# The last four zero pieces as four unequal transfers in a cached-attention training step

## The chip, the cores and the metric

The kernel runs on one core of a Trainium2 chip. The metric is the device time of one execution in microseconds. A measurement is the median of several runs of the kernel before, taken on the same chip as the kernel that it is compared with.

## The reference

Two layers of attention over a cache, each followed by an MLP, for one token of width 1024, forward and backward. The forward pass reads only the last 4096 of 32768 cache rows of each of 4 heads; the gradients of the caches therefore have 28672 rows of zeros for each head, and these must be written as well.

```python
W = min(4096, max(256, Sk // 4))                       # 4096 of Sk = 32768
k = jnp.repeat(k_cache[:, :, Sk - W:, :], rep, axis=1)
v = jnp.repeat(v_cache[:, :, Sk - W:, :], rep, axis=1)
p = _softmax(jnp.einsum("bhqd,bhkd->bhqk", q, k) * (Dh ** -0.5), axis=-1)
...
x = x + _A_ref(_layernorm(x), A_k_cache, A_v_cache, A_wq, A_wo)
x = x + _B_ref(_layernorm(x), B_w1, B_b1, B_w2)        # act = h * tanh(softplus(h))
x = x + _A_ref(_layernorm(x), A_k_cache, A_v_cache, A_wq, A_wo)
x = x + _B_ref(_layernorm(x), B_w1, B_b1, B_w2)
...
_out, _vjp = jax.vjp(_f, A_x, A_k_cache, A_v_cache, A_wq, A_wo, B_w1, B_b1, B_w2)
_grads = _vjp(grad_out)                                # out_1 .. out_8
```

out_2 and out_3 are the gradients of the key and the value cache, (1, 4, 32768, 128) in bf16. out_4, out_5, out_6 and out_8 are the gradients of the weight matrices wq, wo, w1 and w2.

## The kernel before

All matrices are streamed from memory in tiles of 128 partitions, most of them 1 MB (8 KB per partition), by DMAs that SP issues; a small planner (`Ring`) keeps a list of wanted tiles and issues the next one as soon as a slot is free. TensorE computes matrix times vector products and transposes, VectorE and ScalarE evacuate PSUM and compute row products. The weight matrices are passed several times: forward for both layers, backward for both.

The gradients of the weights and of the last 4096 cache rows are outer products. They are made late, in `units_rows`, `units_cols` and `units_kv`: two or four matmuls into a PSUM bank pair, one evacuation by VectorE or ScalarE (`evac`, which picks the engine with the smaller load), and a store of half a stage or the rest of it by SP (`store`, L1050 and L1055). Four lists (`todo`) are served in turn by `work`.

The zeros of out_2 and out_3 are written by POOL's own DMA queue. `zjobs` holds 56 jobs: for each of the two outputs and four heads, the 28672 zero rows are seen as 128 partitions of 224 rows, and these as seven pieces of 4096 elements (8 KB) per partition, 1 MB in all. Half of the first piece is written by SP, the other half goes to the end of the list. `zeros(n, after)` (L257) issues the next n jobs; with `after` given, POOL first copies one element of that tile, so that it waits until the tile is there. The calls stand all along the program: after o of the second forward layer, and at many points of the backward pass. The source is always `zt`, a tile of zeros with 4096 elements on each partition.

The backward pass of the first attention layer is the last pass that reads weights: wo (`do1`), then wq (`dn1(t)`, called for each of the eight row blocks t). In it `zeros(2, dnp[...])` stands at t == 3 (L1219), and the last call, `zeros(4)` (L1228), stands behind the whole pass: three whole pieces and the half. After it no zeros are left; the rest of the program makes and stores gradients.

Other transfers of POOL's queue lie between. `take_back` (L836) reads vectors of the forward pass back from a scratch in memory: AC as two transfers of 28 rows of 256 bytes, then OC (2 x 32 rows), NB and NA (2 x 8 rows each). `rows_go(nc.gpsimd)` (L1041) moves rows inside SBUF: four transfers of 8 rows of 256 bytes, two of 7 rows of 1024 bytes. In the profiled execution they are issued between 276.9 and 304.2 us.

Of the kernel before, what the change touches and what calls it, by code (L numbers as in the profile page):

```python
# [15 lines left out]
P = 128  # L16
HQ = 32
DH = 128
# [3 lines left out]
G = 4  # L22
# [71 lines left out]
def kernel(  # L94
# [22 lines left out]
    nc = tc.nc  # L117
# [3 lines left out]
    ZR = Sk - W  # L121
# [9 lines left out]
    def sb(shape, dtype, name):  # L131
        return keep.tile(shape, dtype, name=name)
# [24 lines left out]
    ZC = 4096  # L157
    zt = sb([P, ZC], BF16, "zt")
# [36 lines left out]
    for hi in range(4):  # L195
        r = slice(32 * hi, 32 * hi + 32)
# [49 lines left out]
    zjobs = []  # L246
    for out_t in (out_2, out_3):
        for g in range(G):
            dst = out_t[0, g, 0:ZR, :].rearrange("(p r) d -> p (r d)", p=P).rearrange("p (r c) -> p r c", c=ZC)
            for k in range(dst.shape[1]):  # L250
                zjobs.append(dst[:, k, :])
    zjobs.reverse()

    pz = sb([1, 16], FP32, "pz")
# [2 lines left out]
    def zeros(n, after=None):  # L257

        if after is not None and zjobs:
            nc.gpsimd.tensor_copy(pz[0:1, pz_n[0] % 16:pz_n[0] % 16 + 1], after[0:1, 0:1])  # L260
            pz_n[0] += 1
        for _ in range(n):
            if zjobs:
                dst = zjobs.pop()
                nc.gpsimd.dma_start(dst, zt[:, 0:dst.shape[1]])  # L265


    KEEP_Q = (5, 6, 7)
# [534 lines left out]
    def last_da(k):  # L803

        for c in (5, 6):
            if k == 0:
                da_dots(c)
            else:
                ring.release(("2", 0, c))
        if k:  # L810
            nc.gpsimd.memset(zt[:], 0.0)
            zeros(1)

    def wo_hook1(c):
        if c == 0:
            zeros(7, OC[:, 0, 1:2])
        if c:
            conv(1)
# [20 lines left out]
    put_by("OC", OC, HQ)  # L839
    put_by("NA", NA, TD)  # L840
    zeros(8, x3)
    sB1 = mlp_fwd(1, x3, st3, lambda: conv(1, "A"))
    put_by("NB", NB, TD)
# [381 lines left out]
            todo[0].append(units_cols(0, 8, out_4))  # L1225

    g0_rest = attn_bwd(0, sA0, g1, ("o", 3), ("q", 3), (), dict(do=do1, dp=dp1, dq=dq1, dn=dn1))
    zeros(4)  # L1228
    stage_free.extendleft(ring_t[:, i, :] for i in range(8))
    stage_free.extendleft(lent)  # L1230

# [50 lines left out]
```

## Time and profile before

| | us |
|---|---|
| median of three runs | 450.59 (450.19 to 450.88) |
| the profiled execution | 450.31 |
| its span, first to last instruction | 448.5 |
| PE busy | 314.8 (70%) |
| DVE busy | 262.2 (58%) |
| ACT busy | 209.4 (47%) |
| POOL busy | 44.5 (10%) |
| DMA: 181.40 MB | 404 GB/s on the mean |
| zeros by POOL: 55 pieces of 1 MB, one of 0.5 MB | first 114.2, last 331.6 (issue) |

The profile is a page with the busy time of each engine, the span in 40 slices with the share of busy DMA engines, the costliest groups of instructions and the DMA issues. The trace behind it answers questions on stretches of time: which instruction ran when, what it waited for, how busy the DMA engines were. It also holds every DMA packet with its start, length, queue and bytes (not its engine), and the 16 steps by which each transfer signals its end, one for each DMA engine.

### The profile page before, as it was taken

Reading aid. Unit: us, or ns where it says so; the run is one execution under the profiler, and the core shown is the slowest. Engines: PE = TensorE matmul, PEld = TensorE weight load, DVE = VectorE, ACT = ScalarE, POOL = GpSimd, SP = SyncE. Lnnn points to the kernel's source line nnn. Section 1 sums busy time; section 2 is a strip of 40 time slices with the busy share of each in tenths; the row PEclk is TensorE's granted clock in tenths of the full one; section 3 lists DMA queues with packets and bytes.
Section 4 is the critical chain, followed back from the end, with each engine's and each line's share of the span. In section 5 each row is a group of like instructions: output and inputs, shape, how many; then the busy total and the mean of one; then the engine's idle time right before and its main releaser. Section 6 shows DMA issues by size and latency. Waiting matters only on the chain.

```text
span 448.5 us, 12849 instructions
## 1 busy us (share of the span) xinstructions
PE 314.8 (70%) x5681; PEld 243.3 (54%) x5681; DVE 262.2 (58%) x516; ACT 209.4 (47%) x238; POOL 44.5 (10%) x94
## 2 busy tenths in 40 slices
PE   3835542565698797987987666798877888899600
PEld 3735532445685696986986545798862222234300
DVE  4504746368551664864477447654478998998600
ACT  2501101011058576861474341561348999999700
POOL 1000000001232212102101003023220000000000
PEclk9955555556559799986799657957685555555555
DMA  8999999999999999999999999999999899999994
GB/s 336 422 420 420 419 419 418 418 355 425 400 422 421 422 422 416 397 422 422 424 422 422 427 423 419 405 410 388 405 397 412 347 411 416 416 420 411 409 406 192
DMA packets 30057, 181.40 MB, mean 404 GB/s; under 512 B 3954, under 2 KB 5162, under 8 KB 12082
## 3 DMA queue, kind: packets, MB, share of 16 engines
q1 hardware_dynamic: 21478, 122.30, 66.6%
q0 software_dynamic: 8432, 58.26, 31.5%
q8 instruction: 44, 0.72, 0.6%
q14 instruction: 11, 0.09, 0.0%
q10 hardware_dynamic: 92, 0.02, 0.0%
HBM read 81.84 MB, written 98.62 MB: 402 GB/s over the span
## 4 chain that ended last, share of the span: by engine, by line
DMA 40%; PE 31%; DVE 13%; ACT 5%; issue 4%; SPq 0%; ACTq 0%; DVEq 0%
DMA ring<-in_B_w_dram 13%; PE BIG L489 10%; DMA W<-in_A_wo_dram 9%; DMA ring<-in_A_wq_dram 7%; DMA ring<-in_A_wo_dram 5%; DMA W<-in_B_w_dram 4%; PE TP L508 4%; PE wide L1129 4%; ACT ring L316 3%; PE wide L1078 3%; DVE ring L313 3%; DMA W<-in_A_k_cache_dram 2%; DVE W L313 2%; PE BIG L667 2%; PE MV L956 2%
## 5 line engine op out<-in xcount | busy, mean ns | idle before, releaser
L316 ACT COPY ring<-BIG 128x1024 bf16<-128x1024 bf16 x52 | 51.4, 1014 | 50.0 <-PE BIG L489 30.2
L1078 PE MATMUL wide<-W 2*128 2x512 bf16 x240 | 53.1, 597 | 9.7 <-ACT ring L316 2.4
L489 PE MATMUL BIG<-ident_bf,ring 128*128 128x128 bf16 x672 | 54.5, 234 | 2.0 <-issue 1.2
L489 PEld LDWEIGHTS <-ring 128*128 128x128 bf16 x768 | 51.6, 107 | 3.4 <-issue 2.7
L466 DVE CUSTOM_DVE_ANT_0 junk<-ring,SC 128x1024 bf16<-128x1024 bf16 x32 | 38.9, 1215 | 11.0 <-DMA ring<-in_B_w_dram 10.6
L1078 PEld LDWEIGHTS <-W 2*128 2x128 bf16 x240 | 12.8, 102 | 46.3 <-issue 45.4
L508 PEld LDWEIGHTS <-ring 128*128 128x128 bf16 x864 | 29.9, 98 | 11.7 <-issue 6.3
L316 ACT CAST ring<-wide 128x1024 bf16<-128x1024 f32 (+1 forms) x37 | 34.5, 1015 | 1.1 <-PE wide L1078 1.1
L265 POOL DMA_DIRECT2D out_dram<-zt x56 | 29.9, 538 | 48.8 <-DMA out_dram<-zt 47.9
L313 DVE CAST ring<-wide 128x1024 bf16<-128x1024 f32 (+1 forms) x27 | 31.3, 1198 | 2.8 <-PE wide L1078 2.7
L316 ACT COPY KT<-BIG 128x1024 bf16<-128x1024 bf16 x22 | 21.6, 1007 | 21.8 <-PE BIG L667 19.9
L313 DVE COPY ring<-BIG 128x1024 bf16<-128x1024 bf16 x32 | 21.8, 689 | 15.1 <-PE BIG L489 12.5
L466 DVE CUSTOM_DVE_ANT_0 junk<-ring,DSX 128x1024 bf16<-128x1024 bf16 x24 | 29.4, 1224 | 0.8
L489 PE MATMUL BIG<-ident_bf,W 128*128 128x128 bf16 x280 | 26.9, 255 | 3.1 <-DMA W<-in_A_wo_dram 2.7
L316 ACT COPY W<-BIG 128x1024 bf16<-128x1024 bf16 x20 | 20.1, 1014 | 11.8 <-PE BIG L489 11.6
L551 PE MATMUL MV<-NA,ring 128*128 128x1 bf16 x512 | 15.3, 165 | 13.4 <-DMA ring<-in_A_wq_dram 12.1
L489 PEld LDWEIGHTS <-W 128*128 128x128 bf16 x288 | 21.6, 123 | 3.5 <-DMA W<-in_A_wo_dram 2.9
L551 PEld LDWEIGHTS <-ring 128*128 128x128 bf16 x512 | 14.7, 104 | 14.2 <-DMA ring<-in_A_wq_dram 12.8
L1129 PE MATMUL wide<-W 32*128 32x256 bf16 x128 | 19.7, 403 | 1.5 <-DVE KT L313 0.9
L316 ACT CAST KT<-wide 128x1024 bf16<-128x1024 f32 x19 | 19.1, 1030 | 1.6 <-PE wide L1129 1.1
L316 ACT CAST W<-wide 128x1024 bf16<-128x1024 f32 x16 | 16.0, 1024 | 6.6 <-PE wide L1078 6.2
L354 PE MATMUL YR<-ring,AC 128*32 128x256 bf16 x208 | 10.9, 367 | 11.1 <-DMA ring<-in_B_w_dram 8.7
(279 smaller groups left out, 524.5 us busy)
## 6 DMA issues: line engine op xcount, KB each, us to landing
out_dram<-zt POOLq DMA_DIRECT2D x55, 1024.0 KB, 20.7
ring<-in_A_wq_dram SPq DMA_DIRECT2D x24, 1024.0 KB, 12.8
ring<-in_A_wo_dram SPq DMA_DIRECT2D x14, 1024.0 KB, 19.0
ring<-in_B_w_dram SPq DMA_DIRECT2D x13, 1024.0 KB, 18.9
W<-in_A_wo_dram SPq DMA_DIRECT2D x10, 1024.0 KB, 19.9
out_dram<-ring SPq DMA_DIRECT2D x15, 512.0 KB, 11.1
W<-in_B_w_dram SPq DMA_DIRECT2D x8, 896.0 KB, 18.4
out_dram<-ring SPq DMA_DIRECT2D x5, 1024.0 KB, 12.3
```

Of the source, the lines that this page charges most:

```text
L265: nc.gpsimd.dma_start(dst, zt[:, 0:dst.shape[1]])
L313: nc.vector.tensor_copy(dst, src)
L316: nc.scalar.copy(dst, src)
L354: nc.tensor.matmul(bank[32 * j:32 * j + 32, 0:n].rearrange("p (g a) -> p g a", a=m.shape[-1]), lhsT=vec.to_broadcast([P, 32]), rhs=m, star ...
L466: nc.vector.tensor_tensor_reduce(out=out, in0=a, in1=vec, scale=1.0, scalar=acc if i else 0.0, op0=ALU.mult, op1=ALU.add, accum_out=acc)
L489: nc.tensor.transpose(b[:, i * P:(i + 1) * P], block(w, i) if block else w[:, i * P:(i + 1) * P], ident_bf[:])
L508: nc.tensor.matmul(out, lhsT=w[:, i * P:(i + 1) * P], rhs=rhs_of(i), start=fresh[0], stop=last and i == n - 1, skip_group_check=True)
L551: nc.tensor.matmul(q_ps[:, h:h + 1], lhsT=ch[:, h * P:(h + 1) * P], rhs=NA[:, t, l:l + 1], start=(k == 0 and h == 0), stop=(k == TD - 1), ...
L667: nc.tensor.transpose(b[:, i * P:(i + 1) * P], T[:, g, 8 * b8 + i, :], ident_bf[:])
L956: nc.tensor.matmul(dq_ps[:, g_ * 8:g_ * 8 + 8], lhsT=KT[:, g_, t, :], rhs=DSX[:, c:c + 8], start=(g_ == 0 and t == 0), stop=(t == TS - 1), ...
L1078: nc.tensor.matmul(b[:, 512 * i:512 * i + 512], lhsT=R[at:at + 2, lo:lo + P], rhs=R[at:at + 2, ro + 512 * i:ro + 512 * i + 512], start=Tru ...
L1129: nc.tensor.matmul(b[:, k * 256:(k + 1) * 256], lhsT=RT[32 * g:32 * g + 32, a, tp, :], rhs=YS[32 * g:32 * g + 32, :], start=True, stop=Tru ...
```

## The change

The seven pieces of the last head of out_3 are cut in another way. The first 512 units of 32 rows (8 KB each, 4 MB in all) are set aside as `zless`; the other 384 units become three whole pieces. The list has 52 jobs then, so the call at t == 3 takes the last whole piece and the half piece, and the last `zeros(4)` becomes `zeros_less()`: four transfers of 4 x 33, 1 x 17, 3 x 33 and 8 x 33 units. Each of the 16 shares reads one partition of `zt` (0, 4, 8, 12; 16; 20, 24, 28; 64, 68 to 92), over and over, and writes one contiguous stretch of the output.

```diff
     zjobs = []
     for out_t in (out_2, out_3):
         for g in range(G):
-            dst = out_t[0, g, 0:ZR, :].rearrange("(p r) d -> p (r d)", p=P).rearrange("p (r c) -> p r c", c=ZC)
-            for k in range(dst.shape[1]):
-                zjobs.append(dst[:, k, :])
+            rest = out_t[0, g, 0:ZR, :]
+            if (out_t, g) != (out_3, G - 1):
+                dst = rest.rearrange("(p r) d -> p (r d)", p=P).rearrange("p (r c) -> p r c", c=ZC)
+            else:
+                units = rest.rearrange("(u r) d -> u (r d)", r=ZC // DH)
+                zless, dst = units[0:4 * P], units[4 * P:].rearrange("(r p) c -> p r c", p=P)
+            zjobs += [dst[:, k, :] for k in range(dst.shape[1])]
     zjobs.reverse()
...
+    def zeros_less():
+
+        at = 0
+        for k, p, n in ((4, 0, 33), (1, 16, 17), (3, 20, 33), (8, 64, 33)):
+            nc.gpsimd.dma_start(zless[at:at + k * n].rearrange("(k n) c -> k n c", k=k),
+                                zt[p:p + 4 * k:4, None, :].to_broadcast([k, n, ZC]))
+            at += k * n
...
     g0_rest = attn_bwd(0, sA0, g1, ("o", 3), ("q", 3), (), dict(do=do1, dp=dp1, dq=dq1, dn=dn1))
-    zeros(4)
+    zeros_less()
```

## The prediction

> **What bounds the kernel now.** I read the page's slices first: the 16 DMA engines are full from start to end, whatever PE, DVE and ACT do.
>
> ```profile
> DMA  8999999999999999999999999999999899999994
> GB/s 336 422 420 420 419 419 418 418 355 425 400 422 421 422 422 416 397 422 422 424 422 422 427 423 419 405 410 388 405 397 412 347 411 416 416 420 411 409 406 192
> ```
>
> From slice 18 on only slice 32 (347 GB/s) and the last (192) lie far under the rest. Next the timeline at the end: the last evacuation ends at 423.6 us, SP issues the last store at 437.7, the span ends at 448.5. The end is the drain of the stores.
>
> ```profile
> 422.61 1.02 ACT L316 CAST W<-wide 128x1024 bf16<-128x1024 f32 x1
> ...
> 437.72 1.06 SPq L1050 DMA_DIRECT2D out_dram<-W  x1
> ```
>
> Then that drain in windows (from:to, length, the engines' busy times and counts, PE clock, DMA share, GB/s):
>
> ```profile
> 440.00:442.00 2.00, 0.00 (x0) 0.00 (x0) 0.00 (x0) 0.00 (x0) 0.00 (x0) 0.50 1.03 410
> 442.00:443.00 1.00, 0.00 (x0) 0.00 (x0) 0.00 (x0) 0.00 (x0) 0.00 (x0) 0.50 0.33 131
> 443.00:444.00 1.00, 0.00 (x0) 0.00 (x0) 0.00 (x0) 0.00 (x0) 0.00 (x0) 0.50 0.06 25
> 444.00:445.00 1.00, 0.00 (x0) 0.00 (x0) 0.00 (x0) 0.00 (x0) 0.00 (x0) 0.50 0.07 29
> 445.00:446.00 1.00, 0.00 (x0) 0.00 (x0) 0.00 (x0) 0.00 (x0) 0.00 (x0) 0.50 0.06 25
> 446.00:447.00 1.00, 0.00 (x0) 0.00 (x0) 0.00 (x0) 0.00 (x0) 0.00 (x0) 0.50 0.07 29
> ```
>
> A share of 0.06 is one engine in sixteen. From about 443.1 to 447.16 (the last packet record) one engine alone moves its part: 4.1 us of the span belong to one late engine, which I call S. 29 packets of 4 KB in that time give 0.155 us per 4 KB, 0.31 us for an 8 KB row.
>
> **Since when S is late.** Each transfer signals its end in 16 steps, one per engine. For the zero piece issued at 327.95 the fifteenth step is at 333.8, the last at 338.9; for the store issued at 436.5 they are 442.2 and 446.3. With zeros alone on the queues (163 to 185 us) the last step advances about 2.75 us per piece, the others 2.45. S therefore loses while zeros run and keeps its lag afterwards: after 355 us no zeros are left, and nothing lets S catch up, since it never idles. The other fifteen do idle:
>
> ```profile
> 352.00:354.00 2.00, 1.59 (x11) 0.46 (x8) 2.00 (x3) 1.79 (x4) 0.00 (x0) 0.50 0.80 309
> 354.00:356.00 2.00, 1.40 (x10) 0.35 (x8) 2.00 (x3) 2.00 (x4) 0.00 (x0) 0.50 0.73 291
> 356.00:358.00 2.00, 1.92 (x10) 0.46 (x10) 1.67 (x3) 2.00 (x3) 0.00 (x0) 0.50 0.71 285
> ```
>
> (0.20 + 0.27 + 0.29) x 2 us = 1.5 us, in which production of stores is the limit. So bytes given to or taken from S move the end at 0.31 us per row, down to the second latest engine (443.1); up to 1.5 us more on each of the others hides in that gap.
>
> **Part 1: the same bytes in another order.** The t == 3 step takes a piece and the half piece instead of two pieces; the four transfers carry 4 MB (512 rows of 8 KB, the diff's units) instead of 3.5 MB. Bytes in total and the count of 56 issues stay. POOL's last issues were
>
> ```profile
> 327.95 2.63 POOL L265 DMA_DIRECT2D out_dram<-zt  x5
> 331.60 0.53 POOL L265 DMA_DIRECT2D out_dram<-zt  x1 [1.02 <-DMA out_dram<-zt]
> ```
>
> and nothing follows on POOL. A transfer of 2 x 32 rows (W<-dr_OC) took 0.70 us to issue against 0.53; even at 1.5 us each the four would be out by 336 us, while earlier pieces keep the engines busy until about 337. Cost 0; without that cover it is the excess of the issue times, about 2 us, most of it inside the 1.5 us gap.
>
> **Part 2: who moves the rows.** Before, a piece has 128 partitions, 8 rows per engine: four pieces are 32 rows on each. The new shapes are 4, 3 and 8 shares of 33 rows, and one transfer of 17 rows. The trace has POOL transfers of both shapes, and the packet records of POOL's queue show where they went:
>
> - One counting dimension: W<-dr_AC, 28 rows of 256 B, came as 512 B on fourteen engines, two rows each, the same fourteen both times. The two seven-row transfers (L1041, 303 us) also came as seven pairs of 1024 B packets, each pair on one engine. I see no rotation in these.
> - Two dimensions, outer 2: W<-dr_OC, dr_NB and dr_NA. S's own sequence between 290.8 and 294.2 us, when only S still had POOL work, is 512, end, 512, end, 64, 64, end, 32, end, 2048, end. The 64 and 32 are fillers that engines without a share get (4 B per row). So S moved no part of OC or NB, but half of NA (2048 B of 4 KB). Three transfers, successive pairs of engines, S in the third.
>
> Applied to the change: the 17 rows have one counting dimension, so two go to each of eight engines and one to a ninth; they start with the engines of the seven-row transfers. S is among those seven (a pair of 1024 B packets at 313.9, after every other engine had signalled by 310.9), so S gets 2. The 4 + 3 + 8 shares go on from the engine behind the NA pair: fifteen engines in succession. One of sixteen stays without 33 rows, the one just before the start: the second engine of the NA pair. S is one of that pair.
>
> S as the first of the pair: 33 + 2 = 35 rows, 3 more than before, 3 x 0.31 = 0.93 us at the end. Fillers add at most 0.15 us (six packets of about 25 ns). Bound below: S now reads its 33 rows from another partition than its own eight; if what slows it by 12% (2.75 against 2.45) is tied to those partitions, it saves up to 0.12 x 33 x 0.31 = 1.2 us. So between -0.2 and +1.1 us; I take +0.9, the row that is measured on S without zeros.
>
> The Trainium skill, page "DMA: Bandwidth & Descriptors", section "Why a DMA increments its semaphore by 16 and not by 1", says that POOL transfers on fewer than 16 engines take successive engines from a rotating position, on as many as divide the outer dimension. By it 17 rows would go to one engine; it names exceptions that are spread over all 16, and the 28-row packets here are such a one. The same page, section "Latency and other measured facts", calls engines 7 and 15 the usual slow ones beside POOL transfers; here one engine is slow, and it took part in seven-row transfers, so I do not rest on that numbering.
>
> **The rivals.**
> 1. Forecast: S keeps a share of 33. No relief; 450.59 + 0.9 = 451.5 (450.4 to 451.7). For it: it holds for S first in the pair, and for either if the six small transfers between NA and the zeros (298 to 304 us) move the start, or if other runs start elsewhere. Against it: S second of the pair is as likely by the NA packets.
> 2. Faster: S is the second engine of the pair and gets 2 rows. 30 rows less are 9.3 us, more than its lag; it is enough from 14 rows less on (4.1 / 0.31). The end falls to the second latest engine, 443.1, whose 3 extra rows (0.9 us) hide in the gap of 1.5: 450.6 - 4.1 = 446.5 (446.0 to 447.4). Place and price are in the 443 to 447 windows.
> 3. The 17 rows stay on one engine that is not S: sixteen engines in succession, S gets 33, one row more: 450.59 + 0.3 = 450.9. The change then does not do what it says for S. Against it: the 28 rows in pairs.
>
> By the page's rule with the rotation starting at S's turn, S would get 17 rows, and the end would fall by the same 4.1 us as in rival 2. For that S would have to be fifth from the start, and the NA packets put it fifteenth or sixteenth.
>
> **How the numbers follow.** The profiled execution took 450.31 (span 448.5 and 1.8 around it), 0.28 under the median 450.59 of three; the differences above are added to the median. A measurement of this kernel tells about 0.2% (0.9 us) from no change. Forecast 0.53: slower 0.47, and 0.06 within 0.2% by the lower bound. Rival 2, which needs one place in the rotation and no shift: 0.39. Rival 3: 0.08, within 0.2%. So faster 0.39, same 0.14, slower 0.47. The predicted time is the forecast's, 451.5; its own range is 450.4 to 451.7. The range has to take in rival 2: 446.2 to 451.9.
>
> **What would show it.** Forecast: the one-engine stretch at the end (share 0.06) stays 4 to 5 us long, and S's last POOL packet comes about 1 us later than 355.05. Rival 2: no such stretch, the DMA share falls from 1 to 0 within about 1 us at 443, and POOL's queue is done on all engines before 350. Rival 3: the stretch is longer by 0.3. In all of them PE, DVE and ACT keep their times. I am wrong throughout if the dip at 352 to 358 or the issue of stores on SP moves by more than 1 us: then the end is not decided by S's bytes.

## The result, and the profile after

The changed kernel takes 458.11 us (median of six runs, 456.87 to 458.67) against 450.74 for the kernel before in the same comparison: ratio 1.016, 95% interval 1.0143 to 1.0177, 7.4 us slower. The forecast was 451.5 and the range ended at 451.9. The profiled execution took 458.43, with a span of 456.7.

The page of the changed kernel, DMA rows of the slices and the queue that POOL writes to (packets, MB, share of 16 engines' span):

```profile
DMA  8999999999999999999999999999999799999994
GB/s 335 423 421 419 418 420 419 421 356 418 398 421 419 416 413 415 391 418 422 426 420 424 410 387 330 405 416 418 421 372 350 267 410 417 415 422 411 408 407 195
q0 software_dynamic: 9536, 58.27, 31.5%
```

Slices 30 to 32, counted from one (331 to 365 us), are the new thing: 372, 350 and 267 GB/s, where before they had 397, 412 and 347 in slices of nearly the same time. (Slice 25 is low too, 330 against 419, but it lies ahead of the changed transfers, and e2 below has 353 there at an unchanged time.) The same stretch and the end in windows of the changed kernel (from:to, length, busy times and counts of PE, PEld, DVE, ACT, POOL, PE clock, DMA share, GB/s):

```profile
334.00:370.00 36.00, 27.87 (x143) 8.12 (x141) 31.41 (x39) 31.32 (x37) 0.36 (x1) 0.50 0.92 333
...
338.00:342.00 4.00, 3.04 (x18) 0.74 (x16) 4.00 (x5) 4.00 (x5) 0.00 (x0) 0.50 0.99 355
354.00:358.00 4.00, 3.00 (x19) 0.74 (x16) 4.00 (x4) 3.79 (x6) 0.00 (x0) 0.50 0.95 333
358.00:362.00 4.00, 3.62 (x15) 0.86 (x15) 3.68 (x5) 4.00 (x5) 0.00 (x0) 0.50 0.75 284
362.00:366.00 4.00, 3.78 (x23) 1.45 (x22) 3.16 (x4) 3.72 (x5) 0.00 (x0) 0.50 0.53 210
366.00:370.00 4.00, 3.14 (x18) 0.78 (x18) 4.00 (x4) 4.00 (x6) 0.00 (x0) 0.50 1.02 405
...
450.00:451.00 1.00, 0.00 (x0) 0.00 (x0) 0.00 (x0) 0.00 (x0) 0.00 (x0) 0.50 0.43 168
451.00:452.00 1.00, 0.00 (x0) 0.00 (x0) 0.00 (x0) 0.00 (x0) 0.00 (x0) 0.50 0.07 29
452.00:453.00 1.00, 0.00 (x0) 0.00 (x0) 0.00 (x0) 0.00 (x0) 0.00 (x0) 0.50 0.06 25
454.00:455.00 1.00, 0.00 (x0) 0.00 (x0) 0.00 (x0) 0.00 (x0) 0.00 (x0) 0.50 0.07 29
```

The kernel before, the same 36 us:

```profile
334.00:370.00 36.00, 29.52 (x142) 8.65 (x142) 31.84 (x35) 33.40 (x39) 0.00 (x0) 0.50 0.97 392
```

From 334 to 370 us 59 GB/s are missing: 59 x 36 = 2.1 MB, and at the 408 GB/s of the stretches around it 5.2 us. The loss has two parts. At 338 to 342 the engines are all busy (share 0.99) and move 355 GB/s: they work more slowly. From 358 to 366 they are idle for a quarter to a half: they have nothing to do. At 366 both are over. By the shares the idle part is the smaller one, (0.97 - 0.92) x 36 = 1.8 us more than before. The one-engine stretch at the end is still there (451 to the last packet at 455.27; 4.3 us against 4.1).

The first part is in the packet records. An 8 KB row of zeros took 351 ns on the mean at 334 to 346 us and 386 at 346 to 366, against 316 and 317 before. The median hardly moved (309 and 314, before 309 and 313): most rows go as fast as before, and some take much longer. Over 400 ns took 10% of the rows at 334 to 346 us (699 ns on their mean) and 38% at 346 to 366, before 0.7% and none. The 4 KB packets of SP's stores went from 162 and 164 ns on the mean to 199 and 176.

The second part is in SP's timeline (start, length, line, operation, count); first before, then after:

```profile
342.11 3.79 SPq L1050 DMA_DIRECT2D out_dram<-W  x3
349.60 0.33 SPq L1050 DMA_DIRECT2D out_dram<-ring  x1
353.26 4.23 SPq L1055 DMA_DIRECT2D out_dram<-ring  x4
```

```profile
346.86 6.09 SPq L1063 DMA_DIRECT2D out_dram<-W  x3
354.98 0.33 SPq L1063 DMA_DIRECT2D out_dram<-ring  x1
359.56 7.02 SPq L1068 DMA_DIRECT2D out_dram<-ring  x4
```

After one store SP issues nothing for some microseconds, although DVE and ACT keep making more. As the semaphores of the issues and their landings show, the transfers of SP (and two small ones of ACT in this stretch) use eight completion semaphores in turn, so a store goes out only when the transfer eight places earlier has landed on all sixteen engines. Before, the store issued at 339.4 landed on its last engine at 353.2, and SP went on at 353.26. After, the store issued at 342.94 landed at 359.5, and SP went on at 359.56; the next landing, 363.9, let the next one go at 363.94. While SP waits, an engine that has emptied its queue has no work.

The profiled execution differs by 8.1 us (458.43 - 450.31). Beside the 5.2 us, its POOL transfers (L1054) are already 1.95 us later at 300.17, before any changed transfer, against 298.22 before; the eight experiments below have them at 297.2 to 298.5. That leaves about 1 us, which would fit three more rows on S. This split is not shown: if the 1.95 us belonged to this execution alone, the others should be shorter by as much, but the profiled execution is only 0.3 us over the median of the six.

### The profile page after: what moved, and what is told of

The parts are those of the page before. It is cut to its first block, busy times and chain, and to the rows that moved or that the text cites. A ratio compares the mean times of both kernels' runs of the same rounds, so it can differ in the third digit from the quotient of the medians.

```text
span 456.7 us, 12849 instructions
## 1 busy us (share of the span) xinstructions
PE 313.5 (69%) x5681; PEld 242.5 (53%) x5681; DVE 261.2 (57%) x516; ACT 209.3 (46%) x238; POOL 45.1 (10%) x94
## 3 DMA queue, kind: packets, MB, share of 16 engines
q0 software_dynamic: 9536, 58.27, 31.5%
## 5 line engine op out<-in xcount | busy, mean ns | idle before, releaser
L502 PE MATMUL BIG<-ident_bf,ring 128*128 128x128 bf16 x672 | 56.1, 239 | 0.9 <-ACT VS L329 0.3
L502 PEld LDWEIGHTS <-ring 128*128 128x128 bf16 x768 | 53.0, 109 | 2.3 <-issue 1.7
L521 PEld LDWEIGHTS <-ring 128*128 128x128 bf16 x864 | 30.4, 98 | 14.4 <-issue 8.1
L329 ACT COPY KT<-BIG 128x1024 bf16<-128x1024 bf16 x22 | 21.7, 1008 | 21.9 <-PE BIG L680 19.8
L269 POOL DMA_DIRECT2D out_dram<-zt x52 | 27.7, 537 | 38.8 <-DMA out_dram<-zt 38.0
L502 PE MATMUL BIG<-ident_bf,W 128*128 128x128 bf16 x280 | 24.1, 236 | 2.5 <-issue 2.3
L564 PEld LDWEIGHTS <-ring 128*128 128x128 bf16 x512 | 14.6, 103 | 12.9 <-DMA ring<-in_A_wq_dram 11.5
L502 PEld LDWEIGHTS <-W 128*128 128x128 bf16 x288 | 19.4, 114 | 3.3 <-issue 3.3
```

Source lines behind the costliest of these rows:

```text
L329: nc.scalar.copy(dst, src)
L502: nc.tensor.transpose(b[:, i * P:(i + 1) * P], block(w, i) if block else w[:, i * P:(i + 1) * P], ident_bf[:])
L521: nc.tensor.matmul(out, lhsT=w[:, i * P:(i + 1) * P], rhs=rhs_of(i), start=fresh[0], stop=last and i == n - 1, skip_group_check=True)
L564: nc.tensor.matmul(q_ps[:, h:h + 1], lhsT=ch[:, h * P:(h + 1) * P], rhs=NA[:, t, l:l + 1], start=(k == 0 and h == 0), stop=(k == TD - 1), ...
```

## The experiments

Four explanations for the 7.4 us stood against each other. **Ports**: with the shares laid from partition 0 on, each engine reads a partition whose reading belongs to another engine, so two engines share one way into SBUF. **Fillers**: 1104 more packets on POOL's queue (9536 - 8432), each 4 bytes. **S's rows**: the late engine has 35 rows, as forecast. **Layout**: contiguous stretches of the output, and the half piece earlier (the expectations call this D).

All edits below are on the changed kernel, in `zeros_less`; k shares from partition p, n rows each. The trace doesn't name the engine of a packet. Engines are numbered here by the partitions that they are taken to read for a transfer of 128: engines 0 to 7 have partitions 0, 4, ... 28 in this kernel's list, engines 8 to 15 have 64, 68, ... 92; e2 and e3 test this.

**e1, the four pieces whole.**

```diff
-        at = 0
-        for k, p, n in ((4, 0, 33), (1, 16, 17), (3, 20, 33), (8, 64, 33)):
-            ...
+        for k in range(4):
+            nc.gpsimd.dma_start(zless.rearrange("(r p) c -> p r c", p=P)[:, k, :], zt[:, 0:ZC])
```

> The new cut of the last head (512 contiguous units set aside, three contiguous pieces, the half piece a step earlier) stays, but the 512 units leave as four whole pieces of 128 partitions. Theory P (ports: in the change most engines read a partition that belongs to another engine's SBUF port, and two engines then share one port): 450.7, within 1 us of before. Theory F (fillers: every engine without a share gets a 4 byte packet per row, 1104 in all, and each takes a turn): 450.7. Theory D (the new order of destinations in memory is slow): 456 to 458.

Measured: 450.52 against 450.77, ratio 0.9995 (0.9986 to 1.0004). The new order, the half piece at t == 3 and the new place in the output cost nothing. The loss is in the shape of the four transfers.

**e2, equal shares, each engine reading its own partition.** The start is read off the small transfers between: OC, NB and NA take two engines each, so with a count from engine 0 the next share goes to engine 6, and the list begins with partitions 24 and 28. That the count begins at engine 0 is an assumption that this run tests.

```diff
-        for k, p, n in ((4, 0, 33), (1, 16, 17), (3, 20, 33), (8, 64, 33)):
+        for k, p, n in ((2, 24, 32), (8, 64, 32), (6, 0, 32)):
```

> Sixteen equal shares of 32 rows as 2 + 8 + 6, with the partitions chosen so that each engine reads its own port if the rotation starts at the engine behind the NA pair (engine 6: partitions 24, 28; 64 to 92; 0 to 20). Destinations as contiguous per engine as in the change, fillers about as many (1024 against 1104). P: 450.7, within 1 us. F and D: 457 to 459, as the change.

**e3, equal shares, each engine reading the partition of the one six places before it.**

```diff
-        for k, p, n in ((4, 0, 33), (1, 16, 17), (3, 20, 33), (8, 64, 33)):
+        for k, p, n in ((8, 0, 32), (8, 64, 32)):
```

> Sixteen equal shares of 32 rows as 8 + 8, partitions 0 to 28 and 64 to 92, so every engine reads the port of the engine six before it, as in the change. Fillers 512, half of the change's. P: 457 to 459. F: about half of the loss, 454. D: 457 to 459. Against e2 it changes only which partition an engine reads (and it has fewer fillers).

Measured: e2 450.86, ratio 1.0001 (0.9992 to 1.001); e3 457.72, ratio 1.0185 (1.0118 to 1.0252), both against 450.77. e3 has four runs, 456.98 to 457.89 and one of 463.05, so its size is less certain than the others'; its lowest is still over 5 us above e2's highest (451.53). Both move 32 rows on every engine in the same contiguous form; for each row e2 has 14 + 8 + 10 fillers, e3 8 + 8, half as many. Windows of e2:

```profile
334.00:370.00 36.00, 29.51 (x146) 8.58 (x142) 32.12 (x34) 33.74 (x39) 0.00 (x0) 0.50 1.02 411
...
354.00:358.00 4.00, 3.24 (x16) 0.92 (x18) 3.67 (x5) 4.00 (x6) 0.00 (x0) 0.50 1.03 413
358.00:362.00 4.00, 4.00 (x23) 1.33 (x19) 3.15 (x4) 3.72 (x5) 0.00 (x0) 0.50 1.01 408
```

Windows of e3:

```profile
334.00:370.00 36.00, 28.85 (x139) 7.96 (x136) 31.37 (x33) 33.06 (x39) 0.00 (x0) 0.50 0.80 306
...
338.00:342.00 4.00, 3.35 (x14) 0.85 (x14) 4.00 (x5) 4.00 (x6) 0.00 (x0) 0.50 1.00 377
354.00:358.00 4.00, 3.10 (x16) 0.82 (x16) 3.67 (x5) 4.00 (x6) 0.00 (x0) 0.50 0.45 164
358.00:362.00 4.00, 3.69 (x21) 1.43 (x21) 3.38 (x4) 4.00 (x6) 0.00 (x0) 0.50 0.24 78
362.00:366.00 4.00, 3.49 (x18) 0.76 (x14) 3.79 (x4) 3.72 (x5) 0.00 (x0) 0.50 0.72 290
```

The only thing that e3 has and e2 has not is the wrong partition (it has one transfer and 512 fillers less), and it carries nearly the whole loss, 6.9 of 7.4 us. In the profile of e3 against that of the kernel before: (392 - 306) x 36 = 3.1 MB, 7.6 us at 408 GB/s, and its profiled execution (457.89) is 7.6 us over that of before. The fillers cost nothing: e2 has 32 x 32 = 1024 of them (its POOL queue has 1008 packets more than before, since it has one transfer less and with it 16 end packets less). In e2 a row took 312 to 322 ns on the mean. In e3 it took 336 at 334 to 346 us, with a median of 309: 8% of the rows took over 400 ns (588 on their mean), in e2 one of 465. So a row from the wrong partition isn't slow by itself; some are, beside the stores.

In e3 most of the loss is the idle part. SP's timeline of e3, and of e2 in the second fence:

```profile
355.19 0.33 SPq L1063 DMA_DIRECT2D out_dram<-ring  x1
360.73 5.23 SPq L1068 DMA_DIRECT2D out_dram<-ring  x4
```

```profile
349.45 0.33 SPq L1063 DMA_DIRECT2D out_dram<-ring  x1
350.39 4.70 SPq L1068 DMA_DIRECT2D out_dram<-ring  x4
```

SP pauses 5.2 us between two stores in e3 (355.52 to 360.73) and 0.6 us in e2.

**e8, half the partitions, each read by two engines.** If the shared way is the cause, a row takes twice as long.

```diff
-        for k, p, n in ((4, 0, 33), (1, 16, 17), (3, 20, 33), (8, 64, 33)):
+        for k, p, n in ((8, 0, 32), (8, 0, 32)):
```

> Sixteen equal shares as in e3, but both transfers read partitions 0 to 28: each of eight ports carries two shares (64 rows, 20 us at 0.31 us per row) and its own engine's stores, eight ports carry none. Theory P: worse than e3, 460 to 470, rows of the zeros at 0.45 to 0.65 us each in their mean. If what costs in e3 is not the port but the mere mismatch of engine and partition: as e3, 457 to 459.

Measured: 458.01 (two runs), ratio 1.0166 (1.0148 to 1.0184). The time is a miss for the ports: it is that of e3, not more, and lies in the range that was given to the mere mismatch of engine and partition. The row decides against the mere mismatch, under which rows would have been those of e3 (median 309). It took 596 ns at the median in 334 to 346 us (559 on the mean), 1.9 times 309, and was expected at 450 to 650. Windows of e8:

```profile
334.00:370.00 36.00, 28.63 (x138) 8.22 (x135) 31.72 (x33) 33.24 (x39) 0.00 (x0) 0.50 1.00 313
...
334.00:338.00 4.00, 2.82 (x16) 0.64 (x14) 3.93 (x4) 4.00 (x5) 0.00 (x0) 0.50 1.07 271
338.00:342.00 4.00, 3.55 (x16) 1.11 (x11) 3.88 (x6) 4.00 (x6) 0.00 (x0) 0.50 0.96 209
358.00:362.00 4.00, 3.69 (x23) 1.46 (x21) 3.37 (x4) 3.72 (x6) 0.00 (x0) 0.50 0.97 388
```

The engines are busy all the time on the mean (1.00; 0.96 to 1.07 in single windows) and move 313 GB/s. So the same seven microseconds are made in another way: e8 loses them to slow packets and shows no idle time, e3 loses less to slow packets and more to SP's wait. The share and the rate together tell the two apart; the time alone doesn't.

The Trainium skill, page "SBUF — State Buffer", section "Door 1: The DMA port swizzle (why [64,N] ≈ [32,N])", says that the 128 partitions lie behind 16 DMA ports of eight partitions each, picked by bits 2 to 4 and bit 6 of the partition. By it e8 reads through eight ports where e2 reads through sixteen; the 596 against 309 ns agree. The two readers in e8 read the same partition, so e8 doesn't tell a shared port from a shared partition, and no other run was made for that. The Trainium skill, page "DMA: Bandwidth & Descriptors", section "The descriptor swizzle", gives the engine of each partition in a transfer of 128 by the same bits. e2's list was made by it, and its ratio of 1.0001 agrees.

**e4, the change with own partitions.** 33 rows on fifteen engines, 17 spread two by two, as in the change; engine 5 is left out. Own partitions hold for the fifteen shares of 33 alone: the 17 rows all come from partition 20, read by nine engines (from partition 16 in the change).

```diff
-        for k, p, n in ((4, 0, 33), (1, 16, 17), (3, 20, 33), (8, 64, 33)):
+        for k, p, n in ((2, 24, 33), (1, 20, 17), (8, 64, 33), (5, 0, 33)):
```

> The change's bytes (33 rows on fifteen engines, engine 5 left out, 17 rows spread two by two over engines 0 to 8), but each engine reads its own port: 2 x 33 from 24, 28; 17 from 20; 8 x 33 from 64 to 92; 5 x 33 from 0 to 16. P, and the late engine is the second of the NA pair (5): 446 to 447.5, the one-engine stretch at the end gone. P, and the late engine is the first of the pair (4, with 35 rows): 451.3 to 452, the stretch 1 us longer. F and D: 457 to 459.

Measured: 451.70, ratio 1.0022 (1.0012 to 1.0031): 0.9 to 1.0 us slower. This is the change as the prediction had it, nearly without what the prediction left out. What is left of it are the 17 rows, as the packet records suggest: at 332 to 340 us eight rows took 0.9 to 2.5 us each, where the longest in e2 and e7, without such a transfer, took 0.55 and 0.44. The end in windows of e4:

```profile
445.00:446.00 1.00, 0.00 (x0) 0.00 (x0) 0.00 (x0) 0.00 (x0) 0.00 (x0) 0.50 0.07 29
447.00:448.00 1.00, 0.00 (x0) 0.00 (x0) 0.00 (x0) 0.00 (x0) 0.00 (x0) 0.50 0.07 29
448.00:449.00 1.00, 0.00 (x0) 0.00 (x0) 0.00 (x0) 0.00 (x0) 0.00 (x0) 0.50 0.02 8
```

One engine alone, now into the 449th microsecond. The stretch isn't 1 us longer, as expected, but begins later too (about 445 to 448.4, 3.4 us against 4.1). Engine 5 had only two rows here, and the stretch stayed, so S is not engine 5.

**e5, 18 rows on engines 4 and 5, 34 on the others; e6, 4 and 36; e7, e5's sizes with the 18 on engines 6 and 7.**

```diff
# e5
+        for k, p, n in ((2, 24, 34), (8, 64, 34), (4, 0, 34), (2, 16, 18)):
# e6
+        for k, p, n in ((2, 24, 36), (8, 64, 36), (4, 0, 36), (2, 16, 4)):
# e7
+        for k, p, n in ((2, 24, 18), (8, 64, 34), (6, 0, 34)):
```

> Own ports as in e4, but engines 4 and 5 carry 18 rows each and the other fourteen 34 (2 x 34 from 24, 28; 8 x 34 from 64 to 92; 4 x 34 from 0 to 12; 2 x 18 from 16, 20). Theory L (the late engine is engine 4, and the end follows its bytes): 14 rows less than 32 are 4.3 us, 446 to 447, and the one-engine stretch at the end is gone. Rival M (another engine or the lanes of SP's stores end last all the same): 449 to 450.5.

> As e5 with 4 rows on engines 4 and 5 and 36 on the others. L: no further gain, since the end is with the others by then: their 2 rows more than in e5 are 0.6 us, 446 to 447.6. M: 449 to 450.5.

> The same sizes as e5, but engines 6 and 7 are the ones with 18 rows, engine 4 has 34 like the rest. L: two rows more on the late engine, 451.2 to 451.8. M, or any engine will do: as e5.

Measured: e5 446.72 against 450.47, ratio 0.9916 (0.9903 to 0.9929), faster than both kernels. e6 446.93, 0.9922 (0.991 to 0.9934), the same as e5: with S out of the way the other engines end last. e7 451.17, 1.0014 (1.0004 to 1.0025), just under the 451.2 of its expectation: its sizes are e5's, but S has two rows more than before, forecast 2 x 0.31 = 0.62 us, measured 0.7. So the gain belongs to one engine; with e4 it is engine 4, the first of the pair that NA's two halves went to. Windows of e5, the former dip and the end:

```profile
354.00:358.00 4.00, 3.55 (x15) 0.89 (x15) 3.67 (x5) 4.00 (x6) 0.00 (x0) 0.50 1.03 409
...
440.00:441.00 1.00, 0.00 (x0) 0.00 (x0) 0.00 (x0) 0.00 (x0) 0.00 (x0) 0.50 0.38 156
441.00:442.00 1.00, 0.00 (x0) 0.00 (x0) 0.00 (x0) 0.00 (x0) 0.00 (x0) 0.50 0.19 78
442.00:443.00 1.00, 0.00 (x0) 0.00 (x0) 0.00 (x0) 0.00 (x0) 0.00 (x0) 0.50 0.06 25
443.00:444.00 1.00, 0.00 (x0) 0.00 (x0) 0.00 (x0) 0.00 (x0) 0.00 (x0) 0.50 0.04 16
```

The share falls from 0.38 to 0.04 within four windows. The stretch of one engine is not quite gone, as was expected: some 1.7 us are left (442 to the last packet at 443.69) of 4.1. The gain is 3.75 us, where 14 rows less were priced at 4.3. The dip at 352 to 358 is gone, with the same work on DVE and ACT.

## Why the prediction was wrong

**The step that failed** is the bound on the other partition: "S now reads its 33 rows from another partition than its own eight". I took that as a possible saving, for S alone, up to 1.2 us. It is a loss, and it falls on every engine: all fifteen shares of 33 read a partition that belongs to an engine five or six places before. Rows went from 316 and 317 ns on the mean to 351 and 386, stores with them, because some rows take much longer while stores run. e3 against e2 prices it at 6.9 us (457.72 - 450.86) with equal shares. No row of the trace before had an engine reading another's partition at this size, so by its own rule the bound should have had a loss on its other side; it had none, and the range ended at 451.9. That the kernel came out slower, as forecast, is luck: the forecast's own cause, three more rows on S, makes about 0.9 of the 7.4 us.

**A second step failed and made the loss larger.** The dip at 352 to 358 was read as "production of stores is the limit". It was SP, which waited for the eighth-last transfer, a store, to land on S (353.2, then 353.26; fifteen engines had it at 349.2). I saw the idle share and the busy DVE and ACT, and did not look at what SP waited for. Read rightly, the dip says that a late landing on one engine stops SP, and that the others idle once their queues are empty: that raises the price of slow packets in this stretch. It needs both. In e4 SP paused 3.7 us as well (348.79 to 352.52), and the share stayed at 0.98:

```profile
350.00:354.00 4.00, 3.00 (x18) 0.86 (x18) 4.00 (x5) 3.80 (x5) 0.00 (x0) 0.50 0.98 387
```

e5 (409 GB/s at 354 to 358) and e2 (413) have no dip there with the same work on DVE and ACT, so production was not the limit.

**Right: the other order costs nothing, who moves the rows, and what they cost on S.** Part 1's cost of 0 is e1's ratio of 0.9995. The 1104 added packets are one filler for each row on each engine without a share, 12 x 33 + 13 x 33 + 8 x 33 = 1089, and 15 more for the 17 rows: two on eight engines and one on a ninth leave seven engines with two fillers and one with one. S as the first of the pair with 35 rows was 3 x 0.31 = 0.93 us; e4 measured 0.9 to 1.0, in which its slow 17 rows can't be told apart, and e7, without them, 0.7 for two rows. The 0.31 stands although the prediction miscounts: of its 29 packets, 25 are of 4 KB and 4 are signals of 4 bytes, and the 4 KB packets follow each other at 0.155 us. The Trainium skill, page "DMA: Bandwidth & Descriptors", section "Why a DMA increments its semaphore by 16 and not by 1", would put the 17 rows on one engine by its rule and two to an engine by its exception; the count of 15 is the exception's.

**Right: the price of rival 2.** It gave 446.5 for S with at least 14 rows less; e5, with 14 less and own partitions, measured 446.72, and e6, with 28 less, 446.93. Its condition was not met by the change, because S was the first of the pair.

**Small: the fillers.** I had put six packets of about 25 ns; there are 1104 of 9 ns, 66 of them on S if it is in the last transfer, and e2, with 64, shows that they cost nothing here.

**The check points.** PE, DVE and ACT kept their times (313.5, 261.2, 209.3 us busy). SP's last store moved from 437.72 to 445.83, and the dip moved and grew. The prediction had named both as what would make it "wrong throughout", and so it was: the end is still S's, but everything ahead of it had moved by some 7 us. The sign for the forecast, S's last POOL packet about 1 us later than 355.05, failed (363.17) but tells nothing of the cost: e2 has it at 363.71 at an unchanged time.

**Open.** Why engine 4 is slower while zeros run (2.75 against 2.45 us per piece) was not tried. The Trainium skill, page "DMA: Bandwidth & Descriptors", section "Latency and other measured facts", names engines 7 and 15 as the usual slow ones; here it is engine 4. How much of the change's own 5.2 us is slow packets and how much is SP's wait can't be split exactly, since the first lengthens the second. What the 17 rows from one partition cost was not tried alone either.

## What to carry to other kernels

When a transfer on fewer than sixteen shares is laid out by hand, choose the source partitions to fit the engines that will get the shares, not the other way round: the same equal shares cost nothing or 1.85%, by that alone. Work out where the rotation stands from the transfers ahead of it, and give the late engine the small share; here that is e5, 0.8% faster than the kernel before. And when engines go idle beside busy producers, look at what the issuing queue waits for before blaming production: here SP, with eight completion semaphores, stopped on the slowest engine of its eighth-last transfer.

## What the runs showed of the hardware

- An 8 KB row read by an engine through another's partitions took 351 to 386 ns on the mean with stores beside it, against 316 before (the median stayed at 309 to 314), and 596 at the median where two engines read each partition, against 309. The 4 KB stores were slowed with them (162 to 199 ns on the mean).
- A busy DMA engine is no measure of work: in e8 the share was 1.00 over 36 us at 313 GB/s, in e2 1.02 at 411.
- A POOL transfer with fewer than sixteen shares gives each other engine one 4-byte packet for every row. 1024 of these cost nothing that can be measured (ratio 1.0001, 0.9992 to 1.001).
- One slow engine of sixteen, engine 4 here, set the end of the kernel by 3.75 us (e5).
- Seventeen rows read from one partition by nine engines probably hinder each other: eight rows of e4 took 0.9 to 2.5 us at 332 to 340 us, where no row of e7 took over 0.44.
